# A unit's last operations over several chunks, and a tile's copying out ahead of the gates' product

## The chip, the cores and the metric

The kernel runs on one core of one Trainium2 chip. The metric is the device time of one execution in microseconds (us). Five engines work side by side, each in the order of its own instruction stream: TensorE (PE; its weight loads are listed apart, as PEld), VectorE (DVE), ScalarE (ACT), GpSimd (POOL) and SyncE (SP), which here only issues DMAs. They wait for each other by semaphores. Times are in us throughout unless a unit is given.

## The reference

Two parts follow each other. The first is a long convolution of u = x * v with a filter made by a small network, and a product with x; the second is a feed-forward layer with the gate h * cos(h).

```python
batch, seq, d_model = (4, 12480, 128)      # x, v: (4, 12480, 128) float32
h_mlp = np.maximum(pos_emb @ w1, 0.0) @ w2
h_filt = h_mlp * np.exp(-0.01 * pos)[:, None]
u = x * v
Uf = np.fft.rfft(u, n=2 * S, axis=1)
Hf = np.fft.rfft(h_filt, n=2 * S, axis=0)
y = np.fft.irfft(Uf * Hf[None, :, :], n=2 * S, axis=1)[:, :S, :]
x2 = (x * y).reshape(B * S, D)             # (49920, 128)
h = x2 @ w_in                              # w_in: (128, 2048), float64 words in memory
g = h * np.cos(h)
out = g @ w_out                            # w_out: (2048, 128)
```

## The kernel before, in words

**The convolution** is done by matrix products: a transform of length 11520 is split as 96 x 120. Per batch of the four there are these stages, each a generator made by `units` (line 609):

- the x * v unit (`u_units`, 641): 30 units of two loads, two products (L441) and sums and differences (L451), on DVE and POOL;
- first transform, "f1" (`f1_units`, 669): 64 units; PE L459, then copies L471 on ACT;
- second transform and product with the filter's spectrum, "f2" (`f2_units`, 680): 48 units; PE `cv<-slots,w`, then four vector operations, L516 and L518 twice each on DVE, each with an addition L519 on POOL behind the L518;
- first inverse transform, "i1" (`i1_units`, 755): 64 units; PE `cv<-even,slots`, a copy L563 on ACT, L565 twice on DVE;
- second inverse transform, "i2" (`i2_units`, 790): 30 units; PE `cv<-slots,tm`, then the product with x (L591 on DVE) and a store to a buffer in memory. `made[0]` counts these units over all batches (120 in all; 30 is `NG`). While i2 of one batch runs, the x * v unit of the next runs inside it (`inverse_units`, 815).

The first batch's f1, f2 and i1 and the filter come before the second part starts, in a stretch of some 280 us; the rest is woven into the second part.

**`units`** runs n units of `parts` pieces each; the evictions and vector operations of unit j (generator `after(j)`) are stepped one per piece while unit j+1's matmuls are issued. Each `yield` tells what the piece costs, in chunks of the second part (`steps / parts`). After the last unit, what is left of its operations is issued at once (lines 632 and 633), and `REST`, 3.0 chunks, is charged.

**The second part** takes tiles of 128 rows (4 x 128 tokens), 98 of them, and for each 16 chunks of 128 hidden columns: 1568 steps in the loop of line 1203. What happens for a chunk (i = step, c = i % 16):

- "up" (`moe_up`, 873): PE multiplies into a bank `ph` of PSUM (L139 `ph<-at,w_in_sb`, recorded as 4 matmuls). ACT rounds it to whole turns (L879), DVE takes the rest (L880, "the sub").
- the gate (`moe_act`, 884), one step later: ACT takes the sine (L885), DVE multiplies it with `ph` (L886, "the product"). The product is the last reader of `ph`; there are 3 such banks, so up of chunk c+3 waits for the product of chunk c. Once the convolution is done, odd chunks take their bank from another pool (`phase_bank`, 869).
- `moe_sums` (888): for each pair of chunks, three operations on POOL.
- "down" (`moe_down`, 901), 7 steps later (`LAG`): products into one of two accumulators, `acca` for even and `accb` for odd chunks (L911; 6 and 8 matmuls in the code, each recorded as two). There is one buffer of each.
- copying a tile out (`moe_evict`, 916): after a tile's down of chunk 14, L925 (ACT) and L926 (DVE) read `acca`; after that of chunk 15, L929, L931 and L932 on DVE read `accb`. With a lag of 7 this falls in the steps with c=5 and c=6 of the next tile.
- turning (`turns`, 1171), from c=10 on: transposes of the tile that comes and of the one that goes out, PE L143, copies L867 and L946 on ACT.

**The order** is the order in which this Python emits instructions. `convolve()` (1155) gives the convolution one chunk's worth of time: it adds 1.0 to `owed` and steps the convolution until the pieces' costs have used it up. In before it is called at the end of every step, except the one in front of the step with a tile's last down (`later`, 1251: c=5); there it is put off to the next step, behind down and the copying out (line 1210), so that two shares fall into c=6. `hurry` (1140) runs the convolution alone where the rows of a tile would not be ready in time, until they are, or until a piece's cost is `REST`.

Of the kernel before, what the change touches and what calls it, by code (L numbers as in the profile page):

```python
# [34 lines left out]
def kernel(  # L35
# [52 lines left out]
    R = S // N2  # L88
# [15 lines left out]
    NFC = DFF // P  # L104
    G = BANK // D
    UA = 2
    NG = N2 // G
# [3 lines left out]
    LAG = 7  # L111
# [24 lines left out]
    def mm(dst, left, right, start=True, stop=True, **how):  # L136
        n = dst.shape[0]
        for lo, hi in ((0, CB), (CB, n)) if tiled[0] else ((0, n),):
            nc.tensor.matmul(dst[lo:hi], left[:, lo:hi], right, start=start, stop=stop, **how)  # L139
# [459 lines left out]
        yield  # L599

    rows_psum = []
    made = [0]
    ot_tiles = []
    zbs = {}

# [3 lines left out]
    def units(n, steps, before, mm, after, parts, ahead=2, skip=0):  # L609


        for j in range(min(ahead, n)):
            for _ in before(j) or ():
                pass
        yield 0.0
        last = iter(())
        for j in range(n):
            early = iter(before(j + ahead) or () if j + ahead < n else ())
            now = None
            for i in range(parts):  # L620
                if i == skip or 2 * (i - skip) == max(parts, 2):
                    now = mm(j, now, int(i > skip))
                if i == 0 and parts == 1:
                    now = mm(j, now, 1)
                next(last, None)
                next(early, None)
                yield steps / parts
            for _ in early:
                pass
            next(last, None)  # L630
            last = after(j, now)
        for _ in last:
            pass
        yield REST

    SOME = range(2, NG, 5)
    REST = 3.0
# [207 lines left out]
    def first_row(n):  # L845
        return min(R + (n - 1) * P, NROWS) if n else 0
# [10 lines left out]
    def moe_turn(n, pt):  # L857
        m = rows_of(n)
        for i in range(G):
            transpose(pt[:, i * m:(i + 1) * m], zbs[n][0:m, i, :], ident)  # L860
# [22 lines left out]

    def moe_act(ph, part, scale):
        nc.scalar.activation(part, part, AF.Sin, scale=scale)  # L885
        nc.vector.tensor_tensor(part, ph, part, op=ALU.mult)  # L886

    def moe_sums(pool, n, gt):
# [12 lines left out]
    def moe_down(n, pair, second, b11, b21, b22, t):  # L901

        r = rows_of(n)
        if pair == 0:
            sums[n, second] = ps_acc.tile([P, 4, P], F32, name="acc" + "ab"[second])
        acc = sums[n, second]
        todo = ((0, 1, t[1]), (1, 4, t[0]), (2, 3, t[3]), (3, 6, b22)) if second else \
            ((0, 0, b11), (2, 2, b21), (1, 5, t[2]))
        for i, (place, weight, right) in enumerate(todo):
            for h in range(2):  # L910
                nc.tensor.matmul(acc[h * CB:(h + 1) * CB, place, 0:r],  # L911
                                 w_out_sb[:, pair, weight, :], right[:, h * r:(h + 1) * r],
                                 start=(pair == 0 and i == 0), stop=(pair == NFC // 2 - 1),
                                 skip_group_check=True)

    def moe_evict(pool, n, second, ot=None):
        r = rows_of(n)
        acc = sums.pop((n, second))

        def twice(a):  # L920
            return bass.AP(tensor=a.tensor, offset=a.offset, ap=[a.ap[0], [0, 2], a.ap[1]])

        if not second:
            ot = ot_tiles[n % 2 if n >= SINGLE else 0]
            nc.scalar.copy(out=ot[:, 2, 0:r], in_=acc[:, 0, 0:r])  # L925
            nc.vector.tensor_tensor(ot[:, 0:2, 0:r], acc[:, 1:3, 0:r], twice(ot[:, 2, 0:r]),  # L926
                                    op=ALU.add)
            return ot
        nc.vector.tensor_tensor(ot[:, 2:4, 0:r], acc[:, 0:2, 0:r], twice(ot[:, 0, 0:r]),  # L929
                                op=ALU.add)  # L930
        nc.vector.tensor_tensor(ot[:, 0, 0:r], acc[:, 1, 0:r], ot[:, 2, 0:r], op=ALU.add)  # L931
        nc.vector.tensor_tensor(ot[:, 2:4, 0:r], acc[:, 2:4, 0:r], ot[:, 2:4, 0:r], op=ALU.add)  # L932
        return ot
# [29 lines left out]
    with tc.manual_schedule():  # L963
        with tc.tile_pool(name="psum", bufs=8, space=PSUM) as psum, \
                ExitStack() as first:
            def bank():
                return psum.tile([P, BANK], F32, name="ps")
# [5 lines left out]
            parts = slots[:, :, 0:2 * N1, :].rearrange("p b (r k) i -> p r k b i", r=2)  # L973
# [144 lines left out]
        def convolutions():  # L1118
            for b in range(B):
                yield from backs[b]  # L1120
                if b == 0:
                    stack.close()
                    tables.__exit__(None, None, None)
                    late = ctx.enter_context(tc.tile_pool(name="late", bufs=1))
                    ot_tiles.append(late.tile([P, 4, P], F32, name="ot_b"))
                    ps_c[0] = stack.enter_context(
                        tc.tile_pool(name="ps_c", bufs=3, space=PSUM))
                if b + 1 < B:
                    yield from forward_units(bank, backs[b + 1])

        tiled[0] = True
        conv = convolutions()
        owed = 0.0

        def load(n):
            while made[0] * R < first_row(n + 1):
                next(conv)
            moe_load(mpool, n)

        def hurry(n):  # L1140

            while made[0] * R < first_row(n + 1):
                if next(conv) == REST:
                    return

        while made[0] == 0:
            next(conv)
# [3 lines left out]
        steps = [(n, c) for n in range(NALL) for c in range(NFC)]  # L1151
        hidden, pairs, gates, ots, obs = {}, {}, {}, {}, {}
        due, turned, taken = False, -3, {}

        def convolve():
            nonlocal owed
            owed += 1.0
            before = count[0]
            while owed > 0.0:
                owed -= next(conv, owed)  # L1160
            taken[i] = count[0] - before
# [2 lines left out]

            return taken[i] and not (taken[i - 1] and taken[i - 2])

        def act(i):
            if i in hidden:
                moe_act(*hidden.pop(i))

        def turns(n):

# [30 lines left out]
        for i in range(len(steps) + LAG):  # L1203
            if i >= LAG:
                pn, pc = steps[i - LAG]
                moe_down(pn, pc // 2, pc % 2, *gates[i - LAG - pc % 2])
                if pc >= NFC - 2:
                    ots[pn] = moe_evict(mpool, pn, pc % 2, ots.get(pn))
                if pc == NFC - 1:
                    convolve()  # L1210
            rest, early = iter(()), False
            if i < len(steps):
                n, c = steps[i]
                if c == 0:
                    due = 0 < n < SINGLE or n % 2
                if n == 0 and c == NFC // 2:
                    load(1)
                soon = n + 2 <= SINGLE or n % 2 == 0
                if c == (NFC - 5 if soon else SOON - 3) and 0 < n < NALL - 2:
                    hurry(n + 2)  # L1220
                if soon and c == (NFC - 2 if n else NFC - 1) and n + 2 < NALL:
                    load(n + 2)
                if n >= SINGLE and n % 2 and c == SOON and n + 2 < NALL:
                    load(n + 2)
                if n == 0 and c == NFC - 2:
                    pt = bank()
                    moe_turn(1, pt)
                    moe_turned(mpool, 1, pt)
                early = due and c >= AT
                if early:  # L1230
                    if n >= SINGLE:
                        act(i - 1)
                    convolve()
                    if n < SINGLE or c == AT + 3 or not just_taken(i):
                        due, turned = False, i
                        rest = turns(n)
                        next(rest)
                ph = phase_bank(c)
                next(rest, None)
                if c % 2 == 0:  # L1240
                    pairs[i] = mpool.tile([P, 2, BANK], F32, name="gt", bufs=4)
                hidden[i] = moe_up(mpool, n, c, pairs[i - c % 2], ph)
            for _ in rest:
                pass
            act(i - 1)
            if i - 4 in pairs:
                gates[i - 4] = moe_sums(mpool, steps[i - 4][0], pairs.pop(i - 4))
            if i == turned + 2:
                for k in sorted(obs):
                    moe_store(k, obs.pop(k))  # L1250
            later = i + 1 >= LAG and steps[i + 1 - LAG:][:1] and steps[i + 1 - LAG][1] == NFC - 1
            if not early and not later:
                convolve()
        for n in sorted(ots):
            moe_store(n, moe_rows(n, ots[n], moe_back(n, ots[n])))
# [28 lines left out]
```

## Time and profile before

| what | us |
|---|---|
| median of 3 runs | 3607.95 (3607.85 to 3608.58) |
| the profiled execution: its time, its span | 3609.1, 3607.3 |
| PE waits for DVE L886 before up (L139 ph), 22 waits recorded | 12.3 (longest 3.6) |
| DVE L880 waits for ACT L879 | 685.1 |
| ACT L879 waits for PE L139 | 1100.0 |
| POOL L894, idle put down to PE accb L911 | 408.3 (longest 39.4) |

The span runs from the first instruction to the last; the time of an execution has a little around it. A wait is idle time of an engine before an instruction, put down to what ended it; a matmul's end in the trace is modelled, so short waits of PE (some tenths of a us) can lie hidden in its busy time and are read from the distance of starts. The pace of PE's products in a row, from starts: up 0.86, down 0.87 for `accb` and 0.65 for `acca`.

Where the stages lie, from the first and last L591, L451, L471, L519 and L565 of each batch:

| stage | batch 1 | batch 2 | batch 3 | batch 4 |
|---|---|---|---|---|
| f1 | before 280 | 535 to 682 | 1353 to 1500 | 2205 to 2353 |
| f2 | before 280 | 697 to 1014 | 1516 to 1832 | 2367 to 2687 |
| i1 | 225 to 276 | 1018 to 1100 | 1837 to 1953 | 2692 to 2818 |
| i2 | 279 to 503 | 1107 to 1327 | 1960 to 2179 | 2824 to 2951 |

From 2951 on the second part runs alone.

### The profile page before, as it was taken

How to read it: one execution, taken by the hardware profiler on the slowest of the kernel's cores; microseconds unless marked ns; L12 is line 12 of the kernel's file. 1: busy time of each engine (PE TensorE's matmuls, PEld its weight loads, DVE VectorE, ACT ScalarE, POOL GpSimd, SP SyncE). 2: the span in 40 equal slices, each digit the busy share in tenths (PEclk: the TensorE clock that was granted, in tenths of full speed). 3: DMA queues.
4: the chain of work that ended last, by engine and by line, in shares of the span. 5: the costliest groups of instructions: out<-in, count | busy, mean ns of one | idle time of the engine just before them, and what ended most of it. 6: DMA issues, size and time to landing. Idle time of an engine off the chain costs nothing.

```text
span 3607.3 us, 102214 instructions
## 1 busy us (share of the span) xinstructions
PE 3554.6 (99%) x40830; PEld 2549.7 (71%) x40830; DVE 2833.4 (79%) x5293; ACT 2232.6 (62%) x4482; POOL 2746.1 (76%) x3236
## 2 busy tenths in 40 slices
PE   8999999999999999999999999999999999999999
PEld 7996767666677777666677776766667876666666
DVE  7888885688887875688877786688887667877877
ACT  7776766656655556666655556665555456667666
POOL 7777985688856996688864897589884458888887
PEclk9999999999999999999999999999999999999999
DMA  7545540122214650022212661022220440000000
GB/s 191 157 147 169 159 117 13 34 72 72 70 32 127 173 139 17 24 76 72 75 30 60 172 171 51 13 64 70 75 63 20 132 125 25 16 22 25 16 22 17
DMA packets 224195, 281.84 MB, mean 78 GB/s; under 512 B 23386, under 2 KB 161122, under 8 KB 223594
## 3 DMA queue, kind: packets, MB, share of 16 engines
q1 hardware_dynamic: 223722, 275.30, 26.7%
q8 instruction: 325, 5.32, 0.6%
q14 instruction: 148, 1.21, 0.1%
HBM read 194.75 MB, written 80.46 MB: 76 GB/s over the span
## 4 chain that ended last, share of the span: by engine, by line
PE 82%; DVE 5%; POOL 2%; ACT 1%; issue 1%; DMA 1%; SPq 0%; ACTq 0%; DVEq 0%; POOLq 0%
PE ph L139 30%; PE accb L911 17%; PE cv L139 17%; PE acca L911 13%; PE cv L459 3%; DVE gt L886 2%; DVE gt L880 1%; PE cv L143 1%; PE ph L143 1%; ACT gt L879 1%; POOL ts L894 1%; DVE xt L441 0%; POOL ts L897 0%; DMA tm<-td 0%; DVE t L518 0%
## 5 line engine op out<-in xcount | busy, mean ns | idle before, releaser
L879 ACT ACTIVATE gt<-ph 128x512 int32<-128x512 f32 (+1 forms) x1376 | 822.0, 597 | 1138.6 <-PE ph L139 1100.0
L880 DVE SCALAR_TENSOR_TENSOR gt<-ph,gt 128x512 f32<-128x512 f32 (+1 forms) x1376 | 946.2, 688 | 658.7 <-ACT gt L879 654.9
L139 PE MATMUL ph<-at,w_in_sb 128*64 128x512 f32 (+2 forms) x5504 | 1424.8, 593 | 14.1 <-DVE gt L886 12.3
L894 POOL TENSOR_TENSOR ts<-gt 128x512 f32<-128x512 f32 (+2 forms) x784 | 999.7, 1275 | 568.0 <-PE accb L911 408.3
L885 ACT ACTIVATE gt<-gt 128x512 f32<-128x512 f32 (+1 forms) x1568 | 975.4, 622 | 26.9 <-DVE gt L880 25.9
L886 DVE TENSOR_TENSOR gt<-ph,gt 128x512 f32<-128x512 f32 (+1 forms) x1376 | 934.6, 679 | 8.8 <-ACT gt L885 7.7
L911 PEld LDWEIGHTS accb<-ts,w_out_sb 128*64 128x64 f32 x9408 | 571.2, 137 | 271.3 <-issue 222.3
L911 PE MATMUL accb<-ts,w_out_sb 128*64 128x128 f32 (+2 forms) x9408 | 653.1, 272 | 1.6 <-DVE ot_a L932 0.2
L898 POOL TENSOR_TENSOR ts<-gt,ts 128x256 f32<-128x256 f32 (+2 forms) x784 | 576.5, 735 | 61.4
L897 POOL TENSOR_TENSOR ts<-ts,gt 128x256 f32<-128x256 f32 (+2 forms) x784 | 575.5, 734 | 61.5
L911 PEld LDWEIGHTS acca<-gt,w_out_sb 128*64 128x64 f32 x6272 | 401.2, 136 | 247.3 <-issue 211.2
L911 PE MATMUL acca<-gt,w_out_sb 128*64 128x128 f32 (+2 forms) x6272 | 480.4, 272 | 0.0
L139 PEld LDWEIGHTS ph<-at,w_in_sb 128*64 128x64 f32 x5504 | 352.0, 137 | 39.9 <-issue 14.7
L911 PE MATMUL acca<-ts,w_out_sb 128*64 128x128 f32 (+1 forms) x3136 | 310.5, 273 | 1.8 <-POOL ts L897 1.4
L911 PE MATMUL accb<-gt,w_out_sb 128*64 128x128 f32 (+1 forms) x3136 | 310.8, 272 | 0.0
L139 PEld LDWEIGHTS cv<-slots,tm 96*40 96x40 f32 (+1 forms) x3840 | 226.1, 125 | 113.8 <-issue 107.7
L519 POOL TENSOR_TENSOR slots<-slots,t 120x256 f32<-120x256 f32 x288 | 210.2, 733 | 69.3 <-DVE t L518 65.8
L139 PE MATMUL cv<-slots,tm 96*40 96x128 f32 (+1 forms) x3840 | 253.8, 273 | 2.8 <-DVE slots L565 1.5
L911 PEld LDWEIGHTS acca<-ts,w_out_sb 128*64 128x64 f32 x3136 | 202.7, 137 | 4.7 <-POOL ts L897 4.3
L139 PEld LDWEIGHTS cv<-even,slots 120*33 120x33 f32 (+1 forms) x3072 | 165.9, 125 | 55.9 <-issue 48.6
L911 PEld LDWEIGHTS accb<-gt,w_out_sb 128*64 128x64 f32 x3136 | 205.0, 137 | 0.0
L139 PE MATMUL cv<-at,w_in_sb 128*64 128x512 f32 (+1 forms) x768 | 198.4, 587 | 0.0
(149 smaller groups left out, 3834.7 us busy)
## 6 DMA issues: line engine op xcount, KB each, us to landing
h<-hd SPq DMA_DIRECT2D x144, 240.0 KB
tm<-td SPq DMA_DIRECT2D x96, 312.0 KB
xt<-in_x_dram SPq DMA_DIRECT2D x120, 208.0 KB
xs<-in_x_dram SPq DMA_DIRECT2D x120, 208.0 KB
zd<-xs SPq DMA_DIRECT2D x119, 208.0 KB
at<-zd SPq DMA_DIRECT2D x96, 256.0 KB
vt<-in_v_dram SPq DMA_DIRECT2D x90, 208.0 KB
w<-wd SPq DMA_DIRECT2D x144, 105.0 KB
```

What stands on the lines that cost most here:

```text
L139: nc.tensor.matmul(dst[lo:hi], left[:, lo:hi], right, start=start, stop=stop, **how)
L143: nc.tensor.transpose(dst, src, ident[0:n, 0:n])
L459: nc.tensor.matmul(dst[lo:hi], u[:, b, lo:hi, i], c1[0:u.shape[0], r:r + 2, :].rearrange("p r k -> p (r k)"), start=True, stop=True)
L519: nc.gpsimd.tensor_tensor(y[:, r], y[:, r], t[:, r], op=op)
L879: nc.scalar.activation(turns, ph[:, 0:m], AF.Identity, bias=phase)
L880: nc.vector.scalar_tensor_tensor(out=part, in0=ph[:, 0:m], scalar=phase, in1=turns, op0=ALU.add, op1=ALU.subtract)
L885: nc.scalar.activation(part, part, AF.Sin, scale=scale)
L886: nc.vector.tensor_tensor(part, ph, part, op=ALU.mult)
L894: nc.gpsimd.tensor_tensor(ts[:, 0:2, 0:half], gt[:, :, half:2 * half], gt[:, 0, 0:2 * half].rearrange("p (h n) -> p h n", h=2), op=ALU.sub ...
L897: nc.gpsimd.tensor_tensor(t[2], t[1], b11, op=ALU.add)
L898: nc.gpsimd.tensor_tensor(t[3], b21, t[2], op=ALU.subtract)
L911: nc.tensor.matmul(acc[h * CB:(h + 1) * CB, place, 0:r], w_out_sb[:, pair, weight, :], right[:, h * r:(h + 1) * r], start=(pair == 0 and i ...
```

## The change

Three edits, and the order that comes of them.

1. `units`: the last unit's remaining operations are stepped one per piece, each charged `steps / parts`, and what they cost is taken off `REST`; at least 2.0 chunks are charged at the end. A counter `ended` tells that a unit's generator came to its end, and `hurry` stops by it rather than by the value `REST`.
2. `moe_act` yields between the sine (ACT) and the product (DVE). In the step with c=5 (`last`) the sine is issued as before, and the product is held back to the next step, behind down and the copying out (L929, L931, L932).
3. The convolution's share at c=5 is put off only where the step is `late`: `last`, and i2 of the second to fourth batch is under way (`NG < made[0] and made[0] % NG`). Elsewhere it is issued at the end of c=5, ahead of the copying out.
4. So in f1, f2, i1 and the first batch's i2 the order on DVE at the end of a tile is: sub of chunk 5, the convolution's operations, L929, L931, L932, product of chunk 4, sub of chunk 6. Before it was: sub of chunk 5, product of chunk 4, L929, L931, L932, the convolution's operations, sub of chunk 6. In the late steps it is the new order with the convolution's operations behind the product.

```diff
     rows_psum = []
-    made = [0]
+    made, ended = [0], [0]
...
             next(last, None)
             last = after(j, now)
+        rest = REST
         for _ in last:
-            pass
-        yield REST
+            yield steps / parts
+            rest -= steps / parts
+        ended[0] += 1
+        yield max(rest, 2.0)
...
     def moe_act(ph, part, scale):
         nc.scalar.activation(part, part, AF.Sin, scale=scale)
+        yield
         nc.vector.tensor_tensor(part, ph, part, op=ALU.mult)
...
         def hurry(n):
 
-            while made[0] * R < first_row(n + 1):
-                if next(conv) == REST:
-                    return
+            done = ended[0]
+            while made[0] * R < first_row(n + 1) and ended[0] == done:
+                next(conv)
...
+        held, late = iter(()), False
...
-        def act(i):
+        def act(i, held=False):
             if i in hidden:
-                moe_act(*hidden.pop(i))
+                acts = moe_act(*hidden.pop(i))
+                next(acts)
+                if held:
+                    return acts
+                for _ in acts:
+                    pass
+            return iter(())
...
                 if pc >= NFC - 2:
                     ots[pn] = moe_evict(mpool, pn, pc % 2, ots.get(pn))
-                if pc == NFC - 1:
+                for _ in held:
+                    pass
+                if late:
                     convolve()
...
-            act(i - 1)
+            last = 0 <= i + 1 - LAG < len(steps) and steps[i + 1 - LAG][1] == NFC - 1
+            held = act(i - 1, last)
...
-            later = i + 1 >= LAG and steps[i + 1 - LAG:][:1] and steps[i + 1 - LAG][1] == NFC - 1
-            if not early and not later:
+            late = last and NG < made[0] and made[0] % NG
+            if not early and not late:
                 convolve()
```

## The prediction

> **What bounds the kernel now.** I read the page first (engine shares, then the waits of the tensor engine, PE), then busy time by stage, then PE and the vector engine (DVE) side by side where the change cuts in.
>
> ```profile
> span 3607.3 us, 102214 instructions
> PE 3554.6 (99%) x40830; PEld 2549.7 (71%) x40830; DVE 2833.4 (79%) x5293; ACT 2232.6 (62%) x4482; POOL 2746.1 (76%) x3236
> ```
>
> PE is busy 99%, so the time is PE's work, which the change leaves as it is (the built program has the same instructions, in another order), plus what PE waits. The waits are where anything can be won or lost. The view of busy time by stage, columns as the first line of the view says, for one second-transform stretch ("f2", 720 to 990), one stretch after the last convolution ("alone", 3060 to 3510) and the place of the longest wait:
>
> ```profile
> core 0: us, PE busy (x) PEld busy (x) DVE busy (x) ACT busy (x) POOL busy (x), PEclk, DMA share, GB/s
> 528.50:532.40 3.90, 3.71 (x24) 2.78 (x26) 2.53 (x5) 1.23 (x3) 1.48 (x3) 0.57 0.73 211
> 720.00:990.00 270.00, 267.83 (x2838) 174.91 (x2836) 236.43 (x470) 162.46 (x297) 240.45 (x285) 1.00 0.24 71
> 3060.00:3510.00 450.00, 449.11 (x4890) 298.47 (x4888) 359.83 (x598) 314.09 (x579) 362.79 (x398) 1.00 0.07 21
> ```
>
> In f2 DVE is busy 236 of 270, 88%: it has little room, and it is where the change moves work. Timeline of DVE (start, length, line, out<-in) in chunks 5 and 6 of tile 36, in f2:
>
> ```profile
> 1580.54 0.68 DVE L880 SCALAR_TENSOR_TENSOR gt<-ph,gt 128x512 f32<-128x512 f32 x1
> 1581.14 0.69 DVE L886 TENSOR_TENSOR gt<-ph,gt 128x512 f32<-128x512 f32 x1
> 1581.73 0.42 DVE L929 TENSOR_TENSOR ot_b<-accb,ot_b 128x256 f32<-128x256 f32 x1
> 1582.19 0.29 DVE L931 TENSOR_TENSOR ot_b<-accb,ot_b 128x128 f32<-128x128 f32 x1
> 1582.51 0.42 DVE L932 TENSOR_TENSOR ot_b<-accb,ot_b 128x256 f32<-128x256 f32 x1
> 1582.85 0.42 DVE L516 TENSOR_TENSOR slots<-cv,h 120x256 f32<-120x256 f32 x1
> 1583.18 0.68 DVE L880 SCALAR_TENSOR_TENSOR gt<-ph,gt 128x512 f32<-128x512 f32 x1
> 1583.78 0.68 DVE L886 TENSOR_TENSOR gt<-ph,gt 128x512 f32<-128x512 f32 x1
> ```
>
> DVE is back to back, with no idle note on any row. Call the first L886 product 4, the second product 5. PE in the same place (up 6, a convolution matmul, acca, up 7, accb, up 8):
>
> ```profile
> 1580.59 1.03 PE L139 MATMUL ph<-at,w_in_sb 128*64 128x512 f32 x4
> 1581.45 0.61 PE L139 MATMUL cv<-slots,w 124*64 124x256 f32 x4
> ...
> 1582.54 1.03 PE L139 MATMUL ph<-at,w_in_sb 128*64 128x512 f32 x4
> 1583.40 0.83 PE L911 MATMUL accb<-ts,w_out_sb 128*64 128x128 f32 x12
> 1584.05 0.39 PE L911 MATMUL accb<-gt,w_out_sb 128*64 128x128 f32 x4
> 1584.52 1.08 PE L139 MATMUL ph<-at,w_in_sb 128*64 128x512 f32 x4
> ```
>
> There are three ph banks, so up 7 needs product 4 and up 8 needs product 5. Product 4 ends at 1581.83, up 7 starts at 1582.54: 0.71 of slack. Product 5 ends at 1584.46 and up 8 starts 0.06 later: PE waited (accb was through by 1583.40+0.87=1584.27).
>
> **The main loss: product 4 behind the copying out.** In the new order DVE does, after the L880 of chunk 5, the convolution's operation of that chunk, then L929, L931, L932, then product 4. The three take 1582.85-1581.73=1.12, a convolution operation 1583.18-1582.85=0.33. Product 4 of tile 36 then ends at 1581.83+1.12+0.33=1583.28; up 7 starts at 1583.33; 0.86 for up 7 and 0.87 for accb put up 8 at 1585.06, not 1584.52: 0.54 lost. Product 5 is not late (the same work lies before it), and accb(15), on which L929 waits, is through at 1580.6 even with a convolution matmul in front, so the copying out does not wait. What is queued behind it on DVE is product 4 alone, and up 7 waits for that; ACT is not held. I did this sum for tiles 34 to 43, where both orders have the same pieces: where a convolution matmul (0.44) lies between up 7 and up 8 (35, 37, 38, 40, 42, 43) the loss is 0.76 to 0.97, in the four others about 0.51; together 7.4, 0.74 a tile. f2 covers chunk 5 of 31 tiles (11 to 21, 34 to 43, 58 to 67): **+22.9**; ends 15.5 (all as the cheap ones) and 30 (all as the dear ones).
>
> The same sum elsewhere. First inverse stage, tiles 1 to 5 (slack before up 7: 0.72, 0.70, 0.05, 2.05, 0.25): 0.4+1.2+1.0+0+0.5=**+3.1**. Tiles 6, 29, 53, with next to no convolution, slack 0.17: 1.1+0.5+0.5=**+2.1**. First transform, 12 tiles, slack 1.56, DVE free but accb 0.87 later because the convolution's matmuls go in front: product 4 ends about 1.65 later, 0.15 each, **+1.8** (0 to 3). Later inverse stages, 15 tiles, where the convolution keeps its place: 1.12 against a slack of about 1.1, **+1.0** (0 to 2). Forced stretches: the dearer unit ends (f2 now costs 3.4+2.0 chunks instead of 3.0, the x * v unit 4.0) delay the convolution, and the three stretches in which it runs without the other product grow from 142 to 167 steps. The longest (1060.1 to 1099.4, 88 steps) has PE busy 38.8 of 39.3, so 25 steps cost 25 x 0.5/88, **+0.2**. Sum of losses 31.1.
>
> **What is won.** Alone: accb of the next tile waits for L932.
>
> ```profile
> 3124.51 1.03 PE L139 MATMUL cv<-at,w_in_sb 128*64 128x512 f32 x4
> 3125.60 0.88 PE L911 MATMUL accb<-ts,w_out_sb 128*64 128x128 f32 x12
> ```
>
> From up 7 to accb are 1.09 where 0.86 is the pace: 0.23. With the copying out ahead of product 4 it ends 0.6 earlier and the wait goes; up 7 takes another pool's bank here, so product 4 being late costs nothing. 24 x 0.23, **-5.5**. Last transform (i1), 5 tiles: two convolution shares in chunk 6 make PE wait 0.65; these waits go, but product 4 is then late by nearly as much: **-0.6** (-3.2 to +1). Ends of f2: waits of 3.3 at 1014-1016, 1832 and 2686 come from last operations issued in one go; **-2.5**. Ends of x * v:
>
> ```profile
> 528.69 1.69 PE L139 MATMUL ph<-at,w_in_sb 128*64 128x512 f32 x4 [3.55 <-DVE gt L886]
> ```
>
> DVE does a memset, two products and two sums here (4.0 from 523.30 to 527.27) in one go. Spread over three chunks they are still all ahead of the product that up waits for, and DVE has about 0.2 to spare per chunk, so PE loses nearly the same in all, in three waits of about one instead of one of 3.55. The granted clock fell to 0.57 in the stretch above only after this one wait (the up took 1.69 for 1.06, accb with it about 1.6 longer together), and stayed 1.00 after all waits of up to 1.3; so I take 0.3+1.6 off, and half of the two waits of 0.9 at 1344 and 2197: **-2.8**. (The Trainium skill, "TensorE: Matmul & The Clock Gate", section "What's actually happening", says that an idle window of about 3.4 us halves the clock until a busy one of that length; this trace agrees, with 3.55 idle. By that rule the 1.6 is saved only if no piece reaches 3.4; else the gain is 1.2.) Start-up: the weights of f2 are made before f1's last unit is through, which takes away a wait of 1.1 at 136.7 (PE on DVE w L332): **-1.1** (0 to -2). After up 8 DVE is ahead by what PE lost, so later waits of these tiles (0.8 at up 9, 2.3 at up 10 and 11 over 30 tiles) shrink: **-2.0** (0 to -4). Sum of gains 14.5.
>
> **Sum.** 31.1-14.5=+16.6. The profiled execution took 3609.1 (span 3607.3 and 1.8 around it): 3625.7. It lies 1.15 above the median 3607.95, which gives **3624.5**.
>
> **Rivals.**
> 1. *The waits add up further* (15%). Late up 7 makes L880 of chunk 7 late, DVE idles, and up 8 and up 9 each wait again: every f2 tile loses 1.12+0.33 less some 0.25 of slack, 1.2 x 31=37 instead of 22.9: 3607.95+16.6+14=3639. For it: DVE at 88%. Against: after up 8 only 0.8 of waits in 30 tiles at up 9.
> 2. *The delay is covered, and the other gains stay: not slower* (13%). Decisive is the slack of up 7: from 1.5 on, product 4 can go behind the copying out free. If PE is already held elsewhere in the new f2 order so that up 7 comes that late, the 22.9 fall out: 3607.95+16.6-22.9=3601.7. For it: f1 and i1 have 1.56 and 2.98. Against: 0.28 to 0.75 measured in f2.
> 3. *Only the stage ends change* (10%), where the chunk-5 order proves neutral in all stages: the gains at ends, -2.5-2.8-1.1, and +0.2: 3601.7 too, without the 5.5 of the alone stretch. Against: the built order has L929 in front of L886 in every tile.
>
> **How the numbers follow.** A measurement of this kernel can tell 0.2%, 7.2 us. My forecast has 62%. Its own range, from the ends of the terms, is 15.5+8.2-17=+7 to 30+8.2-9=+29, 3615 to 3637. The range of 8 in 10 takes in the rival above and part of those below: 3609 to 3640. Slower by over 0.2%: the forecast but for a tail, and rival 1, 78%; within: that tail and most of rivals 2 and 3, 14%; faster by more: 8%.
>
> **What would show it.** In the profile after: waits of PE ph L139 for L886, 12.3 us in all now, grow by some 20, nearly all before up 7 of f2 tiles, with L929 to L932 just ahead of that L886 on DVE; the 0.23 before accb gone in the alone stretch; no 3.55 at the end of x * v and no granted clock of 0.5 there. I am wrong if up 7 starts in f2 without a wait, or if PE's waits grow where no copying out is near.

## The result and the profile after

| kernel | median of the runs | the profiled execution: time, span |
|---|---|---|
| before | 3607.8 (6 runs, 3606.4 to 3608.6) | 3609.1, 3607.3 |
| changed | 3624.8 (6 runs, 3623.2 to 3626.0) | 3623.5, 3621.5 |

The changed kernel is slower: ratio 1.0048, 95% interval 1.0035 to 1.006. The medians differ by 17.0, the two profiled spans by 14.2; what follows accounts for the 14.2.

In the changed kernel's file L880 has become L883 (the sub), L886 L890 (the product), L929, L931, L932 are L933, L935, L936 (copying out of `accb`), and L911 is L915 (down). From its page:

```profile
span 3621.5 us, 102244 instructions
PE 3547.8 (98%) x40830; PEld 2527.1 (70%) x40830; DVE 2835.6 (78%) x5293; ACT 2222.8 (61%) x4482; POOL 2746.1 (76%) x3236
```

The counts of work are those of before; PE's idle time has grown. Its waits (waiting instruction, releaser, total us, times, longest):

```profile
PE ph L139 <- DVE gt L890: 41.9, 50, 3.2
PE ps L143 <- DVE pe L375: 6.1, 3, 4.9
PE cv L143 <- ACT at L870: 4.1, 8, 0.7
```

The first row was 12.3 in 22 waits: PE now waits 29.6 more for products of gates. The place, DVE in tile 36 (f2), chunks 5 and 6, the one that the prediction worked out:

```profile
1590.46 0.68 DVE L883 SCALAR_TENSOR_TENSOR gt<-ph,gt 128x512 f32<-128x512 f32 x1
1591.06 0.41 DVE L516 TENSOR_TENSOR slots<-cv,h 120x256 f32<-120x256 f32 x1
1591.39 0.41 DVE L933 TENSOR_TENSOR ot_b<-accb,ot_b 128x256 f32<-128x256 f32 x1
1591.84 0.29 DVE L935 TENSOR_TENSOR ot_b<-accb,ot_b 128x128 f32<-128x128 f32 x1
1592.16 0.42 DVE L936 TENSOR_TENSOR ot_b<-accb,ot_b 128x256 f32<-128x256 f32 x1
1592.51 0.68 DVE L890 TENSOR_TENSOR gt<-ph,gt 128x512 f32<-128x512 f32 x1
1593.10 0.68 DVE L883 SCALAR_TENSOR_TENSOR gt<-ph,gt 128x512 f32<-128x512 f32 x1
1593.70 0.68 DVE L890 TENSOR_TENSOR gt<-ph,gt 128x512 f32<-128x512 f32 x1
```

DVE has no gap, as before; but product 4 (the first L890) now ends at 1593.19, 2.73 after the sub of chunk 5 (the first row) began; before it was 1.29. Product 5 (the last row) ends 3.92 after that sub began, before as after. PE at the same place (up 6, a convolution matmul, acca, up 7, accb, up 8):

```profile
1590.51 1.03 PE L139 MATMUL ph<-at,w_in_sb 128*64 128x512 f32 x4
1591.37 0.61 PE L139 MATMUL cv<-slots,w 124*64 124x256 f32 x4
...
1593.24 1.08 PE L139 MATMUL ph<-at,w_in_sb 128*64 128x512 f32 x4 [0.60 <-DVE gt L890]
1594.15 0.83 PE L915 MATMUL accb<-ts,w_out_sb 128*64 128x128 f32 x12
...
1595.02 1.03 PE L139 MATMUL ph<-at,w_in_sb 128*64 128x512 f32 x4
```

Up 7 starts 0.05 after product 4 ends, with a wait noted on it; up 8 comes 4.51 after up 6, where it came 3.93 after it: 0.58 lost, and no wait is left before up 8.

Every wait of PE can be sized from the starts in the trace: for each matmul, its start less the earliest that the pace of the one before on the same half of the array (64 columns in the records) allows. This is called a stall below; it includes what a matmul loses to a halved clock. Summed by stage and by step the stalls are 122.4 before and 136.6 after; the difference, 14.2, is that of the spans. Where it lies:

| term of the prediction | predicted | measured |
|---|---|---|
| f2, up 7 and up 8 (the 30 tiles 11 to 20, 34 to 43, 58 to 67) | +22.9 with tile 21 | +31.6 before up 7, -9.7 before up 8: +21.9 |
| later waits of these tiles | -2.0 | -2.6 |
| ends of f2, tile 21 with them | -2.5 | 0.0 |
| first i2 | +3.1 | +1.2 |
| tiles 6, 29, 53 (x * v unit) | +2.1 | +5.8 |
| ends of x * v | -2.8 | -3.1 |
| f1 | +1.8 | -0.4, all of it where f1 begins (c=12 of tiles 29 and 53); 0.0 behind its copying out |
| i1 | -0.6 | -1.8 |
| later i2 | +1.0 | +0.7 |
| alone | -5.5 | -6.5 |
| start-up | -1.1 | -0.8 |
| forced stretches | +0.2 | not told apart |

The gain in the alone stretch, from PE's timeline (up 7, then accb):

```profile
3136.99 1.03 PE L139 MATMUL cv<-at,w_in_sb 128*64 128x512 f32 x4
3137.85 0.83 PE L915 MATMUL accb<-ts,w_out_sb 128*64 128x128 f32 x12
```

0.86 from start to start, the pace; it was 1.09.

The one place where much more was lost than predicted is tile 6. DVE there, then the POOL instructions beside L441, then PE:

```profile
506.62 1.92 DVE L441 TENSOR_TENSOR xt<-xt,vt 104x256 f32<-104x256 f32 x1
508.46 0.41 DVE L933 TENSOR_TENSOR ot_a<-accb,ot_a 128x256 f32<-128x256 f32 x1
...
509.57 0.68 DVE L890 TENSOR_TENSOR gt<-ph,gt 128x512 f32<-128x512 f32 x1
```

```profile
506.30 0.73 POOL L441 TENSOR_TENSOR xt<-xt,vt 104x256 f32<-104x256 f32 x1
506.99 1.27 POOL L898 TENSOR_TENSOR ts<-gt 128x512 f32<-128x512 f32 x1
```

```profile
510.31 1.08 PE L139 MATMUL ph<-at,w_in_sb 128*64 128x512 f32 x4 [3.25 <-DVE gt L890]
...
512.77 1.93 PE L139 MATMUL ph<-at,w_in_sb 128*64 128x512 f32 x4
```

The x * v product L441 now stands ahead of the copying out and took 1.92, on a tile for which the prediction had 1.1 of loss in all. Up 7 waited 3.25, and right behind that wait the granted clock was halved (busy time by stretch; the last three columns are the granted clock, the DMA share and GB/s):

```profile
510.20:514.20 4.00, 3.89 (x24) 2.39 (x26) 2.54 (x5) 1.12 (x2) 1.47 (x2) 0.64 0.10 33
```

The next up took 1.93 for 1.06. So the halved clock did leave the end of x * v, as predicted, but it moved to tile 6.

### The profile page after: what moved, and what is told of

It is laid out like the page before. It is cut to its first block, busy times and chain, and to the rows that moved or that the text cites. A ratio compares the mean times of both kernels' runs of the same rounds, so it can differ in the third digit from the quotient of the medians.

```text
span 3621.5 us, 102244 instructions
## 1 busy us (share of the span) xinstructions
PE 3547.8 (98%) x40830; PEld 2527.1 (70%) x40830; DVE 2835.6 (78%) x5293; ACT 2222.8 (61%) x4482; POOL 2746.1 (76%) x3236
## 4 chain that ended last, share of the span: by engine, by line
PE 82%; DVE 6%; ACT 1%; issue 1%; DMA 1%; POOL 1%; SPq 0%; ACTq 0%; DVEq 0%; POOLq 0%
PE ph L139 30%; PE accb L915 17%; PE cv L139 17%; PE acca L915 12%; PE cv L459 3%; DVE gt L890 2%; DVE gt L883 1%; PE cv L143 1%; ACT gt L882 1%; PE ph L143 1%; DVE t L518 1%; DVE slots L516 0%; DMA tm<-td 0%; DVE ot_a L936 0%; POOL ts L898 0%
## 5 line engine op out<-in xcount | busy, mean ns | idle before, releaser
L883 DVE SCALAR_TENSOR_TENSOR gt<-ph,gt 128x512 f32<-128x512 f32 (+1 forms) x1376 | 946.1, 688 | 669.9 <-ACT gt L882 667.1
L139 PE MATMUL ph<-at,w_in_sb 128*64 128x512 f32 (+2 forms) x5504 | 1417.9, 593 | 42.7 <-DVE gt L890 41.9
L898 POOL TENSOR_TENSOR ts<-gt 128x512 f32<-128x512 f32 (+2 forms) x784 | 999.3, 1275 | 563.9 <-PE accb L915 337.6
L890 DVE TENSOR_TENSOR gt<-ph,gt 128x512 f32<-128x512 f32 (+1 forms) x1376 | 933.8, 679 | 6.7 <-ACT gt L888 5.6
L915 PEld LDWEIGHTS accb<-ts,w_out_sb 128*64 128x64 f32 x9408 | 563.1, 136 | 252.4 <-issue 223.1
L915 PE MATMUL accb<-ts,w_out_sb 128*64 128x128 f32 (+2 forms) x9408 | 646.4, 272 | 0.0
L915 PEld LDWEIGHTS acca<-gt,w_out_sb 128*64 128x64 f32 x6272 | 391.8, 136 | 259.3 <-issue 221.7
L915 PE MATMUL acca<-gt,w_out_sb 128*64 128x128 f32 (+2 forms) x6272 | 475.4, 272 | 0.0
L139 PEld LDWEIGHTS ph<-at,w_in_sb 128*64 128x64 f32 x5504 | 342.7, 137 | 67.1 <-DVE gt L890 46.6
L915 PE MATMUL acca<-ts,w_out_sb 128*64 128x128 f32 (+1 forms) x3136 | 305.1, 272 | 1.2 <-POOL ts L901 1.0
L915 PE MATMUL accb<-gt,w_out_sb 128*64 128x128 f32 (+1 forms) x3136 | 304.9, 272 | 0.0
L139 PEld LDWEIGHTS cv<-even,slots 120*64 120x64 f32 (+1 forms) x3072 | 164.7, 125 | 55.3 <-issue 51.4
L915 PEld LDWEIGHTS acca<-ts,w_out_sb 128*64 128x64 f32 x3136 | 198.1, 137 | 2.5 <-POOL ts L901 2.0
L915 PEld LDWEIGHTS accb<-gt,w_out_sb 128*64 128x64 f32 x3136 | 199.0, 137 | 0.0
```

What stands on the lines that cost most here:

```text
L883: nc.vector.scalar_tensor_tensor(out=part, in0=ph[:, 0:m], scalar=phase, in1=turns, op0=ALU.add, op1=ALU.subtract)
L898: nc.gpsimd.tensor_tensor(ts[:, 0:2, 0:half], gt[:, :, half:2 * half], gt[:, 0, 0:2 * half].rearrange("p (h n) -> p h n", h=2), op=ALU.sub ...
L915: nc.tensor.matmul(acc[h * CB:(h + 1) * CB, place, 0:r], w_out_sb[:, pair, weight, :], right[:, h * r:(h + 1) * r], start=(pair == 0 and i ...
```

## The experiments

The theory: PE stands still in f2 because product 4 comes behind more work on DVE than the slack of its bank allows. The main rival: the convolution's early share is what costs, whatever becomes of the product. The first four kernels undo one part or do one part alone. Each time is set beside runs of the kernel before on the same chip.

### The product follows its sine again

```diff
-            held = act(i - 1, last)
+            held = act(i - 1)
```

> The changed kernel, but the product of chunk 4 follows its sine at once again (the copying out comes behind it); the convolution's early share and the spread unit ends stay. Theory (the product behind the copying out is past the slack of up 7): the waits before up 7 of f2 tiles, 32 us of stalls at c=7, go, the waits before up 8 (10 us) and the 0.23 to 0.28 before accb in the alone stretch (6.5 us) come back; about 3600 us, 7 below the kernel before, from i1 (-3.4), ends of x * v (-3) and start-up (-0.8). Rival (the early share is what costs, since it puts convolution operations ahead on DVE and PE): still about 3620 or more.

Measured: 3601.6 (3600.0 to 3603.4) beside 3607.4; ratio 0.9985 (0.9977 to 0.9994). PE's wait for the product:

```profile
PE ph L139 <- DVE gt L890: 7.7, 15, 2.2
```

41.9 fell to 7.7. In f2 the stalls before up 7 are 3.4 (32.1 with the hold) and before up 8 6.2; the 6.7 of the alone stretch is back. With the early share and the spread ends in place, the hold alone makes 23 us of difference; the rival is wrong.

### The hold alone

```diff
+                for _ in held:
+                    pass
                 if pc == NFC - 1:
                     convolve()
...
+            held = act(i - 1, last)
```

> The kernel before with the held product alone: the product of chunk 4 behind L929, L931, L932 in every tile, the convolution's share where it was (behind both), unit ends as before. Theory: product 4 comes 1.12 us later instead of 1.12 plus 0.33 for each convolution operation, so an f2 tile loses 0.38 on the mean of the ten summed tiles: +11.7 in f2, less 2 regained, +3 in the first i2 and the x * v tiles, +0.7 in the later i2, -6.5 alone: 3614 to 3616 us. Rival (the early share costs): the loss is not here, 3601 us.

Measured: 3613.9 (3612.4 to 3617.2), ratio 1.0018 (1.0009 to 1.0027). Stalls in f2 grew by 9.0 in all (before up 7 from 0.5 to 20.5, before up 8 from 10.2 to 1.0), for 9.7 expected; alone fell by 6.5. So the loss grows with what DVE does ahead of product 4, once that is past the slack: 1.12 of copying out gives 9 in f2; 1.12 and the convolution's operations give 19 (28.4 to 47.6 in the changed kernel, the ends of f2 included).

### The spread unit ends alone

```diff
+        rest = REST
         for _ in last:
-            pass
-        yield REST
+            yield steps / parts
+            rest -= steps / parts
+        ended[0] += 1
+        yield max(rest, 2.0)
```

> The kernel before with the spread unit ends alone (last operations one per piece, at least 2.0 chunks at the end, hurry by the counter). Theory: the work is the same and only waits at ends move; start-up -0.8, ends of x * v -2 to -3 (unless another long DVE operation lands there), ends of f2 0 to -3: 3602 to 3606 us. Rival (the longer charge and the longer forced stretches cost): 3610 us or more.

Measured: 3605.1 (3603.9 to 3607.3), ratio 0.9994 (0.9985 to 1.0003). As expected by the medians, but the interval holds no change, so a gain of this part by itself is not shown; that it does no harm of more than 0.03% is. The stalls of its profile are 4.5 below those of before.

### The early share alone

```diff
-                if pc == NFC - 1:
+                if late:
                     convolve()
...
-            if not early and not later:
+            late = later and NG < made[0] and made[0] % NG
+            if not early and not late:
```

> The kernel before with the early share alone: the convolution's share at c=5 is not put off, except in the later i2; the product follows its sine. Theory: the double share at c=6 of i1 (3.4 us of waits) goes, f2 keeps its 10 us before up 8 because the same DVE work lies before product 5: 3603 to 3606 us. Rival (the early share costs): 3620 us or more.

Measured: 3605.4 (3603.5 to 3607.1), ratio 0.9995 (0.9986 to 1.0004). The 3.5 of stalls at c=6 of i1 are gone, f2 has 9.7 before up 7 and up 8 (10.7 before), only divided otherwise: 3.4 and 6.3. The share costs nothing here, and its gain too lies within the interval.

### Another bank for chunk 7

```diff
-        late = made[0] == B * NG and c % 2
+        late = made[0] == B * NG and c % 2 or c == 7 and made[0] >= NG
```

> The kernel before, with one change: from the second batch on, chunk 7 takes its PSUM bank from the convolution's pool, so that the three ph banks serve one chunk less and up 7 waits for no product, up 8 for product 4 instead of product 5. Theory (the banks tie PE to the products): the 10 us of waits before up 8 in f2 tiles go, the rest stays: 3596 to 3599 us. Rival (PE is held there by something else, or the convolution's three banks run short when one is lent): no gain or slower, 3607 or more.

> The changed kernel with the same lent bank for chunk 7. Theory: product 4 being late hurts only through up 7's bank; with another bank the waits at c=7 go: 31.6 in f2, 3.9 at ends of f2, some 7 in the x * v tiles with the halved clock after tile 6, 3 in i1 and the later i2, not those of the first i2 (3.7): 3624 less 45, 3578 to 3585 us, below the kernel before with the lent bank. Rival (the order itself costs, whatever bank is used): 3610 us or more.

Measured: 3670.1 (ratio 1.0174, 1.016 to 1.0188) for the kernel before with it, and 3658.2 (1.0139, 1.0125 to 1.0153) for the changed one. Both missed what I expected by far. The waits of PE in the changed kernel with the lent bank:

```profile
PE cv L139 <- DVE t L518: 27.1, 17, 2.8
PE cv L139 <- DVE slots L565: 20.3, 16, 2.0
PE ph L139 <- DVE gt L890: 9.4, 14, 2.2
```

The last row, 41.9 without the lent bank, is what the theory said would go. But the convolution's matmuls now wait for L518 and L565, the readers of its own banks, 47 in these two rows: with one of three lent, the convolution stands where up 7 stood. The granted clock was also halved six times in the first of these kernels and four times in the second, against once before. With the lent bank the changed order came out 12 below the other (3658 against 3670), where with the own bank it is 17 above. That does not show the order to be free on another bank: the convolution's own waits differ by 7.5 of the 12, 54.9 in these two rows of the first kernel and 47.4 in the second. A clean fourth bank was not tried; the kernel's pools have two accumulators, three `ph` and three for the convolution.

### The hold only where nothing waits for the bank

After the last convolution up 7 takes a bank of the other pool. First the kernel before with the hold there alone, then the changed kernel with the hold there alone.

```diff
-            held = act(i - 1, last)
+            held = act(i - 1, last and made[0] == B * NG)
```

> The kernel before, with the product held behind the copying out only after the last convolution (made[0] at 120). Theory: the wait of accb for L932 goes in 23 or 24 tiles and nothing else changes: -5.5 to -6.5, 3601 to 3602 us. Rival (the gain seen there belongs to something else): 3607 us.

> The changed kernel, with the product held only after the last convolution. Theory: the kernel without any holding (3601.6) less the 6.5 of the alone stretch: 3594 to 3597 us, faster than both kernels. Rival as for the run before: 3601.6 us.

Measured: 3600.1 (3599.7 to 3602.8), ratio 0.9981 (0.9972 to 0.999); and 3594.5 (3593.2 to 3597.7), ratio 0.9966 (0.9953 to 0.9978), beside 3607.1. The second is as expected, the first gained some 1 more than expected: the same hold that costs some 22 in the f2 tiles of the changed kernel (by the stalls with and without it) gains 6.5 to 7 in the alone stretch.

### No hold in f2, hold elsewhere

```diff
-            held = act(i - 1, last)
+            held = act(i - 1, last and not in_f2[0])
```

> The changed kernel with one exception: in f2 the product follows its sine. Theory: f2's waits are those of the kernel without holding (3.4 before up 7 and 6.2 before up 8, not 32.1 and 0.5), 22 to 23 us less, and the 3.9 before up 7 at the ends of f2 only in part: 3600 to 3604 us; what is then left above 3594.5 is the first i2, the x * v tiles, i1 and the later i2. Rival (the loss is spread over the stages): 3612 or more.

Measured: 3601.1 (3599.5 to 3602.2), ratio 0.998 (0.9971 to 0.9989). Of the 30 us between the changed kernel and the one with the hold in the alone stretch only (3594.5), f2 has some 24. The other 6.7 are, by the stalls of the two profiles (whose spans differ by 7.7), mostly the 3.9 of tile 6, where up 7 waits 3.24 again and the clock was halved for 6.8 around the end of that wait. The first i2 has 0.5, i1 0.8 and the later i2 0.5; 1.7 lie in f2, at single steps other than up 7 and up 8.

### The share of c=5 put off to c=13 in f2

With the hold in the alone stretch only. In f2 the convolution gets no share at c=5 and two at c=13.

```diff
+            if last and in_f2[0]:
+                skipped += 1
+                taken[i] = 0
-            if not early and not late:
+            elif not early and not late:
                 convolve()
+            if skipped and i % NFC == 13:
+                skipped = 0
+                convolve()
```

> The last kernel (product held only after the last convolution, the rest as changed), and in f2 the convolution's share at c=5 is left out and given as a second share at c=13, away from the copying out. Theory (what stands on DVE between the sub of chunk 5 and products 4 and 5 is what PE waits for in f2): product 5 comes 0.33 to 0.66 us earlier, most of the 9.6 us of waits before up 7 and up 8 in f2 go: 3594.5 less 5 to 9, 3586 to 3590 us. Rival (the double share at c=13 makes PE wait there instead): 3594 or more.

Measured: 3599.7 (3598.2 to 3603.4), ratio 0.9978 (0.997 to 0.9987): some 5 worse than without, the rival's side, though not by its mechanism. Before up 7 and up 8 the stalls fell from 9.5 to 5.6, less than expected, but at c=9 they rose from 4.0 to 11.2, and 2.8 came at c=13 of i1, where a share carried over from f2 falls. Part of those at c=9 is this row, 0.9 in 2 waits in the list of before and absent from the list of the kernel this one was built on:

```profile
PE cv L143 <- DMA at<-zd: 4.1, 4, 1.7
```

The transposes of the next tile wait for its load. Why the load comes later, and the rest of the 7 at c=9, was not settled.

### The last sums of x * v on POOL

The best kernel so far (the hold in the alone stretch only) still has one DVE burst ahead of a product: the last two sums of the second batch's x * v, 2.2 in a row.

```diff
             yield from u_units(b, u, engine, place, 1, lambda j: 2 * (
-                nc.vector if b == 1 and j == H // UA - 1 else nc.gpsimd,))
+                nc.gpsimd,))
```

> The changed kernel with the product held only after the last convolution, and the last sums of the second batch's x * v (L451, 2.2 us on DVE in one go, right ahead of a product that up waits for) on POOL, as all other sums. Theory (what stands on DVE ahead of a product is what PE waits for): the wait of 2.2 before up of step 113 goes, and f1's first matmul then waits for POOL, up to 1: 3594.5 less 1 to 2, 3592.5 to 3593.5 us. Rival (POOL is behind by as much, so f1 waits the whole time): 3594.5 or more.

Measured: 3591.9 (3591.0 to 3592.3) beside 3607.3, ratio 0.9956 (0.9943 to 0.997). The longest wait of up for a product went from 2.2 to 1.0, as the theory has it; the time is 0.6 below the range. This is the fastest kernel of the study, 0.44% below the one before and 33 us below the changed one.

## Why the prediction was right, point by point

**What bounds.** That only PE's waits count held: the sum of the stalls worked out from starts moves by 14.2, as the span does.

**Product 4 behind the copying out, +22.9.** Right in place, mechanism and size. The two tests that move product 4 (no hold; hold without the early share) gave a loss that grows with the work put ahead of it: over all steps of the 30 f2 tiles, -3 without the hold, +9 with the hold alone and +19 in the changed kernel, against before. Per tile the sum gave 0.74, measured (31.6-9.7)/30=0.73; in tile 36 0.54 against 0.58. Its core was to set the new end of the product against the slack of the bank, and to take off what PE already waited before up 8.

**The same sum elsewhere.** Too large for the first i2 and f1: there was no loss in f1, where I had product 4 a little later than up 7 comes, and in the first i2 waits at c=8 and c=9 shrank by 1.5 and 1.0, which I had not allowed for (with the early share alone that of c=8 shrank, with the hold alone both). Too small for x * v, and this is the worst-sized term: the DVE product L441 in tile 6 took 1.92, which made a wait of 3.25 out of one of about 1 and brought the halved clock. Not all of that is the hold's: from its first up to that of the next tile, tile 6 takes 30.0 before, 35.6 in the changed kernel and still 32.8 in the changed kernel without the hold, where L441 delays the copying out and `accb` waits for it.

**Gains.** Alone was right in mechanism (shown by the hold in this stretch alone) and somewhat small, 0.23 a tile where starts give 0.28. For the ends of f2, -2.5 came out as nothing: the old waits of 3.3 went, but tiles 21, 44 and 68, whose chunk 5 falls at these ends once f2 is stretched, took 3.9 before up 7. I had counted tile 21 only. The ends of x * v gave 3.1 of 2.8.

**The rivals.** That the waits add up further (3639) did not happen: after up 8, f2 had 2.6 less than before. That the delay is covered (3601.7) fails on the slack; it is what happens where up 7 takes another bank, in the alone stretch. That the order of chunk 5 is neutral fails with the hold alone.

**The sum.** The terms gave +16.6 against 14.2 between the profiles and 17.0 between the medians. Part of the closeness is chance: the errors of the f1 and first i2 terms (-4.1), of the x * v tiles (+3.7) and of the ends of f2 (+2.5) nearly cancel. The forecast of 3624.5 lies still closer to the median of 3624.8, and that is chance too: the profiled execution of before lies 1.3 above its median and that of the changed kernel 1.2 below its own, which makes some 17 out of some 14. The range of 3615 to 3637 does not come out of the terms as stated: with every term at its end it would be 3609 to 3639 (15.5+5.4-20=+0.9 to 30+10.4-9.8=+30.6).

## What to carry to other kernels

An instruction moved ahead on an in-order engine delays all that it passes, so set the delay against the slack of each buffer that a passed instruction frees: the time from its end now to the start of the next user. The same swap gained 6.5 us where the next user took another bank and lost some 22 where the slack was 0.3 to 0.75, so an order may have to differ by stage; a test per stage costs one line. A buffer lent to one user is taken from another: look at the lender's own waits before.

## What the runs showed of the hardware that was not expected

**A DVE operation that reads two SBUF operands is stretched by POOL.** L441 on DVE (104x256) took 0.41 to 0.42 in the six cases of the second part in which nothing ran on POOL beside it, and never less than 1.29 in the 28 cases of the changed kernel (29 of the kernel before, up to 2.84) in which a POOL L898 (L894 before) of 1.27 overlapped it for over 1.0. In every one of these it ended 0.28 to 0.29 after that POOL instruction: here DVE gets on only when POOL is through. In tile 6 it stood behind two POOL instructions in a row, L441 and L898. The gate's product L890, one operand of which lies in PSUM, took 0.67 to 0.69 in all 499 cases of the changed kernel in which L898 overlapped it for over 0.5. The Trainium skill, "GPSIMD Engine Reference", section "Key points", says that POOL shares its SBUF interfaces with VectorE, with contention for DVE instructions with two SBUF inputs; the trace agrees, and gives the size, which decided the wait in tile 6. This was read from three profiles (before, changed, without the hold), not tested by moving the POOL operation.

**The clock can halve without one long idle stretch, and need not.** In the kernel with the spread ends alone and in the one without the hold, the waits at the end of x * v are the same, 0.27, 0.6 and 2.2. With the spread ends:

```profile
525.15 1.08 PE L139 MATMUL ph<-at,w_in_sb 128*64 128x512 f32 x4 [0.58 <-DVE gt L889]
...
529.11 1.58 PE L139 MATMUL ph<-at,w_in_sb 128*64 128x512 f32 x4 [2.22 <-DVE gt L889]
```

Without the hold:

```profile
526.50 1.08 PE L139 MATMUL ph<-at,w_in_sb 128*64 128x512 f32 x4 [0.57 <-DVE gt L890]
...
530.46 1.08 PE L139 MATMUL ph<-at,w_in_sb 128*64 128x512 f32 x4 [2.23 <-DVE gt L890]
```

In the first the up behind the wait took 1.58 for 1.06, and the granted clock in the stretch behind it (530 to 534) was 0.63:

```profile
530.00:534.00 4.00, 4.00 (x30) 3.01 (x28) 1.44 (x3) 1.12 (x2) 0.75 (x1) 0.63 0.73 222
```

In the second it stayed full. The records of the clock lie a whole number of 3.413 apart (the first full stretch is 518.826 long in the kernel before, 152 times that), so they form a grid of windows. Laid over PE's records, the grid tells the two cases apart. The 13 profiles of this study have 17 places, before the end of PE's work, at which the clock was halved; in the window ahead of each of them PE was busy for 0.10 to 0.44 of the window. In the other windows at full clock, over 13000 of them, that share is never below 0.45. Above, PE was busy for 1.19 of the 3.41 ahead of the halved clock (526.13 to 529.54), and for 1.56 in the kernel without the hold (526.67 to 530.08), because its wait of the same length lay across the end of the window. Where the clock stayed halved for a second window (three places), PE was busy for 0.58 to 0.65 of the first; elsewhere for 0.94 or more. These shares rest on modelled ends of matmuls and on one execution of each kernel, and no run moved a wait within its window to test it.

The prediction reckoned with 3.4 of idle as what halves the clock, and with pieces of about one. The waits of 3.25 in tile 6 and 2.22 here are shorter than 3.4, and the clock was halved behind both. Waits cut into pieces of one to two thus do not keep the clock safely: they did at the end of x * v in the changed kernel, without the hold and with the hold in the alone stretch only, and not here.
